# Splitting the last accumulator of an attention kernel into its two banks, with ScalarE normalising one and two output tiles moved ahead

## The chip, the cores and the metric

The kernel runs on 1 core of one Trainium2 chip. The metric is device time in microseconds (us) of one execution. Engines: PE multiplies matrices (PEld is its weight load), DVE is VectorE, ACT is ScalarE, POOL is GpSimd, SP issues the transfers. The granted clock was 1.0. Times of different kernels are compared only with runs of the kernel before on the same chip.

## The reference

Attention of a layer-normed x over given key and value caches, times a gate; 32 heads, 2048 queries, 2048 keys, head width 128, model width 512.

```python
xn = layernorm(x)                                   # x: 1 x 2048 x 512
q  = (xn @ wq) as 32 heads of 128
p  = softmax(q k^T / sqrt(128)); o = p v            # k_cache, v_cache: 32 heads x 2048 x 128
s  = o @ wo                                         # 4096 -> 512
g  = silu(relu(xn W_gate) * (xn W_up) @ W_down)
out = x + s * g                                     # bf16
```

## The kernel before

The kernel handles 128 blocks (32 heads times 4 groups of 512 queries). A block has 8 key pairs: two score matmuls (512 columns), one exponential of 128x1024 on ACT, and, three pairs later, eight value matmuls (129 columns; the extra column sums the weights) into two accumulator banks in PSUM. Each finished block is divided by its sums on DVE and transposed by a transfer. The output projection is done in 16 tiles of 128 rows. For the last four heads it is done at the end, "final tiles" 0 to 15: four matmuls on PE, then on DVE a multiply by the gate and an add to a prepared base, then a transfer out. Tiles 0 to 7 are done inside the pair loop, 8 to 15 behind it. Tiles 12 to 15 need the very last block, which PE transposes itself; a transposing transfer takes 2.4 us from issue to landing in the median.

These are the parts that matter; `j` runs over the four 128-query groups, and bank = j // 2. Left out: everything ahead of the last loop.

```python
def emit_PV_tile(gp, tt):
    b, h, Q, p = blk_of(gp)
    pb = gp % NPB
    vb = h % 2
    if tt == 0:
        if p == 0:
            if gp == 0:
                _wait(pe, tok_pool)
            if Q == 0:
                _wait(pe, v_tok(h))
        pe.wait_ge(sem_exp.h, gp + 1)
    t = 2 * p + tt
    for j in range(4):
        bank = j // 2
        if t == 0 and j % 2 == 0:
            _wait(pe, norm_tok[b - 1][bank] if b >= 1 else acc_free[bank])
        o_ap = ps_acc[:, bank, (j % 2) * 256:(j % 2) * 256 + VW]
        ins = pe.matmul(o_ap, PT[pb][:, tt, j * 128:(j + 1) * 128], V_sb[vb][:, t, 0:VW],
                        start=(t == 0 and j % 2 == 0), stop=(t == KT - 1 and j % 2 == 1))
        if b == NBLK - 1 and t == KT - 1 and j == 1:
            tx = sem_pv.sig(ins)
        if t == KT - 1 and j == 3:
            ty = sem_pv.sig(ins)
    if t == KT - 1:
        if Q == QB - 1 and h + 2 < H:
            _wait(sp, ty)
            issue_v(h + 2)
        if b < NBLK - 1:
            ntok = emit_norm_block(b, ty)
            norm_tok[b] = (ntok, ntok)
        else:
            emit_norm_last(b, 0, tx)
            emit_norm_last(b, 1, ty)

def emit_norm_last(b, bank, pvtok):
    h, Q = divmod(b, QB)
    g, hh = divmod(h, G)
    ob = b % NON
    _wait(dve, pvtok)
    o_ap, z_ap = acc_view()
    js = slice(2 * bank, 2 * bank + 2)
    rtok = sem_rz.sig(dve.reciprocal(rz_sb[:, js, :], z_ap[:, js, :]))
    _wait(dve, rtok)
    tok = sem_norm.sig(
        dve.tensor_tensor(Onorm[ob][:, js, :], o_ap[:, js, :],
                          rz_sb[:, js, :].to_broadcast([128, 2, Dh]), ALU.mult))
    emit_last_transposes(hh, Q, ob, bank, tok)
    return tok

# ... (emit_last_transposes only appends to pending_last)
def flush_last_transposes():
    s = ring_acquire()
    for k, (hh, Q, ob, bank, tok) in enumerate(pending_last):
        tp_ps = ps_r[:, 2 * s + k, :].bitcast(BF16)
        _wait(pe, tok)
        ins = None
        for jj in range(2):
            j = 2 * bank + jj
            ins = pe.transpose(tp_ps[:, jj * 128:(jj + 1) * 128], Onorm[ob][:, j, :], ident[:])
        ptok = sem_ptr.sig(ins)
        _wait(act, ptok)
        c0 = Q * NQ + bank * 256
        last_ot[bank] = sem_otc.sig(
            act.copy(OT_store[(NG - 1) % 2][:, hh, c0:c0 + 256], tp_ps[:, 0:256])
        )
    ring_tok[s] = list(last_ot.values())
```

```python
def emit_final_tile(n, bank):
    Q, j = divmod(n, 4)
    if n == 0:
        _wait(pe, wo_tok(gL))
    if j == 0:
        _wait(pe, (sem_tl[Q], sem_tl[Q].n))
    if Q == QB - 1:
        _wait(pe, last_ot[j // 2])
    ins = None
    for hh in range(G):
        ins = pe.matmul(ps_r[:, bank, 0:D], OT_store[gL % 2][:, hh, n * 128:(n + 1) * 128],
                        Wo_sb[gL % 2][:, hh, :], start=(hh == 0), stop=(hh == G - 1))
    otok = sem_op.sig(ins)
    fb = fin_cnt[0] % NFT
    fin_cnt[0] += 1
    _wait(dve, otok)
    _wait(dve, fin_free[fb])
    mtok = sem_opa.sig(
        dve.tensor_tensor(fin_tmp[fb][:], ps_r[:, bank, 0:D], g_sb[:, n, :], ALU.mult))
    flush_final_add()
    fin_pending.append((n, fb, mtok))
    return mtok

def flush_final_add():
    if not fin_pending:
        return
    n, fb, mtok = fin_pending.pop()
    Q, j = divmod(n, 4)
    _wait(dve, mtok)
    if n == 0:
        _wait(dve, base_done[NT - 1])
    ftok = sem_opa.sig(
        dve.tensor_tensor(x_sb[:, n, :], x_sb[:, n, :], fin_tmp[fb][:], ALU.add))
    fin_free[fb] = ftok
    if Q == QB - 1 or j % 2 == 1:
        n0 = n if Q == QB - 1 else n - 1
        _wait(sp, ftok)
        sem_out.sig(sp.dma_start(out_t[:, n0:n + 1, :], x_sb[:, n0:n + 1, :]))
```

The PSUM ring that `emit_M` takes its banks from has three slots of two banks. The order at the end of the program is set by these lines; LAG is 3, TOTP 1024, NT 16:

```python
for step in range(LAG, TOTP + LAG):
    gp = step
    gq = step - LAG
    bq, hq, Qq, pq = blk_of(gq)
    items = plan.pop((bq, pq), None)
    if gp < TOTP:
        b, h, Q, p = blk_of(gp)
        if p == 0 and Q == 0:
            sp_head_start(h)
        open_S_pair(gp)
        emit_S_tile(gp, 0)
        if items:
            emit_S_tile(gp, 1)
    if items:
        emit_M(items)
    emit_PV_tile(gq, 0)
    if gp < TOTP and not items:
        emit_S_tile(gp, 1)
    emit_PV_tile(gq, 1)

assert not plan
for n in range(NT - 8, NT - 4, 2):
    emit_M([(emit_final_tile, n), (emit_final_tile, n + 1)])
    if n == NT - 8:
        flush_last_transposes()
for n in range(NT - 4, NT, 2):
    emit_M([(emit_final_tile, n), (emit_final_tile, n + 1)])
flush_final_add()
sp.wait_ge(sem_out.h, sem_out.n)
```

The softmax here doesn't subtract the row's maximum and nothing guards it: scores larger than these inputs give would overflow.

## Time and profile before

| | before |
|---|---|
| time, median of 3 runs | 1286.27 us (1286.2 to 1286.35) |
| span of the profiled run | 1284.5 us |
| PE busy | 1266.6 us, 99% |
| DVE busy | 380.5 us, 30% |
| ACT busy | 1001.7 us, 78% |

The page of the kernel before opens with the busy time of each engine, its share of the span and its instructions; its fourth part is the chain of work that ended last, by engine.

```profile
PE 1266.6 (99%) x11813; PEld 835.2 (65%) x12040; DVE 380.5 (30%) x685; ACT 1001.7 (78%) x1109; POOL 13.2 (1%) x25
...
PE 85%; ACT 12%; issue 1%; DVE 1%; DMA 0%; DVEq 0%
```

PE is busy all the time and carries the chain. The change touches only the last 15 us. The timeline lists instructions in order: start, duration, engine, source line, operation, destination <- sources, count. First PE in the tail of the kernel before, from tiles 6 and 7, the last two inside the pair loop:

```profile
1269.96 1.89 PE L774 MATMUL ps_r<-Wo_sb,OT_store 128*128 128x512 bf16 x8
1271.68 1.98 PE L737 MATMUL ps_acc<-V_sb,PT 128*128 128x129 bf16 x32
1273.71 1.67 PE L774 MATMUL ps_r<-Wo_sb,OT_store 128*128 128x512 bf16 x7
1275.22 0.39 PE L709 MATMUL ps_r<-ident,Onorm 128*128 128x128 bf16 x4
1275.45 5.34 PE L774 MATMUL ps_r<-Wo_sb,OT_store 128*128 128x512 bf16 x24
```

L774 is a final tile, L737 the value matmuls, L709 the transposes. Each group starts a little before the end of the one before it: the record of a 512-column matmul lasts 0.379 us, while the next one starts 0.216 us after it. PE has no gap. (The group at 1273.71 has 7 of its 8 records.) DVE in the same stretch:

```profile
1273.59 0.17 DVE L688 RECIPROCAL rz_sb<-ps_acc 128x2 f32<-128x2 f32 x1 [0.60 <-PE ps_acc L737]
1273.79 0.42 DVE L691 TENSOR_TENSOR Onorm<-ps_acc,rz_sb 128x256 bf16<-128x256 f32 x1
1274.13 0.16 DVE L688 RECIPROCAL rz_sb<-ps_acc 128x2 f32<-128x2 f32 x1
1274.33 0.42 DVE L691 TENSOR_TENSOR Onorm<-ps_acc,rz_sb 128x256 bf16<-128x256 f32 x1
1274.67 0.68 DVE L782 TENSOR_TENSOR fin_tmp<-ps_r,g_sb 128x512 bf16<-128x512 f32 x1
1275.26 0.42 DVE L798 TENSOR_TENSOR x_sb<-x_sb,fin_tmp 128x512 bf16<-128x512 bf16 x1
1275.60 0.68 DVE L782 TENSOR_TENSOR fin_tmp<-ps_r,g_sb 128x512 bf16<-128x512 f32 x1
...
1276.53 0.68 DVE L782 TENSOR_TENSOR fin_tmp<-ps_r,g_sb 128x512 bf16<-128x512 f32 x1
...
1281.19 0.69 DVE L782 TENSOR_TENSOR fin_tmp<-ps_r,g_sb 128x512 bf16<-128x512 f32 x1
1281.79 0.75 DVE L798 TENSOR_TENSOR x_sb<-x_sb,fin_tmp 128x512 bf16<-128x512 bf16 x2
```

L688 and L691 are the reciprocals and normalisations of the last block, L782 a final multiply (tile 8 at 1274.67, tile 15 at 1281.19), L798 a final add (the add of one tile follows the multiply of the next). From 1274.67 on DVE starts a tile every 0.93 us, though PE makes one every 0.86 us, so DVE ends its work behind PE: the last multiply starts 0.40 us after PE's end at 1280.79.

### The profile page before, as it was taken

What the parts mean: (1) busy time and instruction counts of PE and PEld (TensorE: products, weight loads), DVE (VectorE), ACT (ScalarE), POOL (GpSimd) and SP (SyncE); (2) the same over time, 40 slices, a digit from 0 to 9 for tenths busy, and PEclk for the clock granted to TensorE, in tenths of its full rate; (3) what the DMA queues carried; (4) which work ended last, traced back from release to release, by engine and by line L of the source; (5) the groups of instructions that cost most, each with busy time, mean ns of one, the idle gap of its engine ahead of it and who ended that gap; (6) DMA issues with size and microseconds to landing.
All of it is one profiled execution on the core that took longest, in us unless ns stands there. A gap on an engine that the chain in (4) does not pass through costs nothing.

```text
span 1284.5 us, 26708 instructions
## 1 busy us (share of the span) xinstructions
PE 1266.6 (99%) x11813; PEld 835.2 (65%) x12040; DVE 380.5 (30%) x685; ACT 1001.7 (78%) x1109; POOL 13.2 (1%) x25
## 2 busy tenths in 40 slices
PE   9999999999999999999999999999999999999998
PEld 5444466676666666666666666666666666666665
DVE  6433311112222222222222222222222222224355
ACT  3322399998888888888888888888888888888884
POOL 2100000000000000000000000000000000000000
PEclk9999999999999999999999999999999999999999
DMA  9600123232222332332221322323323322332202
GB/s 263 131 1 1 22 47 55 60 56 37 36 54 46 71 54 50 55 70 51 54 45 32 67 46 54 55 67 55 55 51 70 54 36 38 51 67 55 49 15 75
DMA packets 240977, 72.13 MB, mean 56 GB/s; under 512 B 227808, under 2 KB 240864, under 8 KB 240864
## 3 DMA queue, kind: packets, MB, share of 16 engines
q1 hardware_dynamic: 240048, 69.76, 28.5%
q8 instruction: 96, 1.57, 0.5%
q10 hardware_dynamic: 816, 0.66, 0.2%
q14 instruction: 17, 0.14, 0.0%
HBM read 32.77 MB, written 2.10 MB: 27 GB/s over the span
## 4 chain that ended last, share of the span: by engine, by line
PE 85%; ACT 12%; issue 1%; DVE 1%; DMA 0%; DVEq 0%
PE ps_acc L737 32%; PE ps_r L640 25%; ACT PT L650 12%; PE ps_r L573 9%; PE ps_r L594 8%; PE ps_acc L506 4%; PE ps_r L487 4%; PE ps_r L483 4%; PE ps_r L774 1%; DVE fin_tmp L782 0%; PE ps_r L397 0%; DMA x_sb<-in_A_x_dram 0%; DVE x_sb L798 0%; ACT gr_sb L449 0%; PE ps_acc L359 0%
## 5 line engine op out<-in xcount | busy, mean ns | idle before, releaser
L650 ACT ACTIVATE PT<-ps_r 128x1024 bf16<-128x1024 f32 x1024 | 952.5, 1054 | 167.7 <-PE ps_r L640 164.9
L737 PE MATMUL ps_acc<-V_sb,PT 128*128 128x129 bf16 x8192 | 776.5, 220 | 10.7
L737 PEld LDWEIGHTS ps_acc<-V_sb,PT 128*128 128x128 bf16 x8192 | 621.1, 98 | 241.7 <-ACT PT L650 3.5
L640 PE MATMUL ps_r<-QT_sb,KT_sb 128*128 128x512 bf16 x1837 | 675.1, 379 | 0.3
L667 DVE RECIPROCAL rz_sb<-ps_acc 128x4 f32<-128x4 f32 x127 | 23.3, 183 | 729.8 <-PE ps_acc L737 729.8
L640 PEld LDWEIGHTS ps_r<-QT_sb,KT_sb 128*128 128x128 bf16 x2048 | 195.0, 98 | 1.1 <-DVE QT_sb L584 0.4
L573 PE MATMUL ps_r<-xnT,Wq_sb 128*128 128x512 bf16 x511 | 130.9, 379 | 0.1
L594 PE MATMUL ps_r<-Wo_sb,OT_store 128*128 128x512 bf16 x447 | 114.4, 379 | 0.1
L584 DVE CAST QT_sb<-ps_r 128x512 bf16<-128x512 f32 x128 | 88.5, 692 | 48.1 <-PE ps_r L573 48.1
L573 PEld LDWEIGHTS ps_r<-xnT,Wq_sb 128*128 128x128 bf16 x512 | 49.9, 97 | 60.6 <-ACT PT L650 27.1
L670 DVE TENSOR_TENSOR Onorm<-ps_acc,rz_sb 128x512 bf16<-128x512 f32 x127 | 87.8, 691 | 4.4
L594 PEld LDWEIGHTS ps_r<-Wo_sb,OT_store 128*128 128x128 bf16 x448 | 43.8, 98 | 52.9 <-ACT PT L650 0.2
L449 ACT ACTIVATE gr_sb<-ps_r 128x512 bf16<-128x512 f32 x56 | 32.9, 595 | 49.6 <-PE ps_r L483 49.1
L607 DVE TENSOR_TENSOR s_acc<-s_acc,ps_r 128x512 f32<-128x512 f32 x96 | 66.0, 687 | 17.4 <-PE ps_r L594 17.4
L455 DVE TENSOR_TENSOR hT<-gr_sb,ps_r 128x512 bf16<-128x512 bf16 x56 | 38.4, 685 | 46.8 <-PE ps_r L487 42.2
L506 PE MATMUL ps_acc<-Wd_sb,hT 128*128 128x512 bf16 x220 | 48.8, 379 | 0.2
L487 PE MATMUL ps_r<-xnT,Wu_sb 128*128 128x512 bf16 x164 | 42.7, 379 | 0.2
L483 PE MATMUL ps_r<-xnT,Wg_sb 128*128 128x512 bf16 x165 | 42.6, 379 | 0.2
L506 PEld LDWEIGHTS ps_acc<-Wd_sb,hT 128*128 128x128 bf16 x224 | 21.9, 98 | 26.4
L514 ACT ACTIVATE sig_sb<-ps_acc 128x512 f32<-128x512 f32 x12 | 7.2, 597 | 29.5 <-PE ps_acc L506 29.5
L487 PEld LDWEIGHTS ps_r<-xnT,Wu_sb 128*128 128x128 bf16 x168 | 16.4, 98 | 19.8
L483 PEld LDWEIGHTS ps_r<-xnT,Wg_sb 128*128 128x128 bf16 x168 | 16.4, 98 | 19.8
(50 smaller groups left out, 181.0 us busy)
## 6 DMA issues: line engine op xcount, KB each, us to landing
V_sb<-in_A_v_cache_dram SPq DMA_DIRECT2D x32, 512.0 KB, 4.8
Wq_sb<-in_A_wq_dram SPq DMA_DIRECT2D x32, 128.0 KB, 2.5
Wo_sb<-in_A_wo_dram SPq DMA_DIRECT2D x8, 512.0 KB, 4.9
OT_store<-Onorm SPq DMA_TRANSPOSE x127, 2.4
Wd_sb<-in_B_W_down_dram SPq DMA_DIRECT2D x1, 1792.0 KB, 14.6
x_sb<-in_A_x_dram SPq DMA_DIRECT2D x3, 512.0 KB, 12.1
out_dram<-x_sb SPq DMA_DIRECT2D x6, 256.0 KB, 2.2
Wg_sb<-in_B_W_gate_dram SPq DMA_DIRECT2D x1, 768.0 KB, 10.3
```

The source lines that it names most:

```text
L455: dve.tensor_tensor(hT[par][:, fc, :], gr_sb[gk][:], ps_r[:, gb + 1, :], ALU.mult)
L483: ins = pe.matmul(ps_r[:, gb, :], Wg_sb[:, c, fs], xT[:, c, xs], start=(c == 0), stop=(c == DC - 1))
L487: ins = pe.matmul(ps_r[:, gb + 1, :], Wu_sb[:, c, fs], xT[:, c, xs], start=(c == 0), stop=(c == DC - 1))
L506: ins = pe.matmul(ps_acc[:, jb, 0:D], hT[par][:, fc, j * 128:(j + 1) * 128], Wd_sb[:, fc, :], start=(fc == 0), stop=(fc == FC - 1))
L573: ins = pe.matmul(ps_r[:, bank, :], Wq_sb[b][:, c, :], xnT[:, c, qs], start=(c == 0), stop=(c == DC - 1))
L584: etok = sem_qpe.sig(dve.tensor_copy(QT_sb[b][:, qs], ps_r[:, bank, :]))
L594: ins = pe.matmul(ps_r[:, bank, 0:D], OT_store[g % 2][:, hh, n * 128:(n + 1) * 128], Wo_sb[g % 2][:, hh, :], start=(hh == 0), stop=(hh == ...
L607: dve.tensor_tensor(s_acc[:, n, :], s_acc[:, n, :], ps_r[:, bank, 0:D], ALU.add)
L640: ins = pe.matmul(ps_r[:, 2 * s + tt, :], KT_sb[h % 2][:, t * 128:(t + 1) * 128], QT_sb[h % 2][:, qs], start=True, stop=True)
L650: act.activation(PT[pb][:], ps_r[:, 2 * s:2 * s + 2, :], ACTF.Exp, scale=scale)
L670: dve.tensor_tensor(Onorm[ob][:], o_ap, rz_sb[:].to_broadcast([128, 4, Dh]), ALU.mult))
L737: ins = pe.matmul(o_ap, PT[pb][:, tt, j * 128:(j + 1) * 128], V_sb[vb][:, t, 0:VW], start=(t == 0 and j % 2 == 0), stop=(t == KT - 1 and j ...
```

## The change

The intent: at the very end, bank 0 (query groups 0 and 1) gets its 12 remaining value matmuls before bank 1, so that its normalisation can start early; ACT, which is out of exponentials by then, does that normalisation in place of DVE; and final tiles 8 and 9 are moved ahead of these value matmuls, tile 10 between them and the transposes, to keep PE busy. The order of the pair loop does not change; the diff of it only takes out the conditions for its last three steps.

```diff
--- before.py
+++ after.py
@@ -686,6 +686,14 @@
             o_ap, z_ap = acc_view()
             js = slice(2 * bank, 2 * bank + 2)
             rtok = sem_rz.sig(dve.reciprocal(rz_sb[:, js, :], z_ap[:, js, :]))
+            if bank == 0:
+                _wait(act, rtok)
+                for j in range(2):
+                    tok = sem_otc.sig(
+                        act.activation(Onorm[ob][:, j, :], o_ap[:, j, :], ACTF.Copy,
+                                       scale=rz_sb[:, j, 0:1]))
+                emit_last_transposes(hh, Q, ob, bank, tok)
+                return tok
             _wait(dve, rtok)
             tok = sem_norm.sig(
                 dve.tensor_tensor(Onorm[ob][:, js, :], o_ap[:, js, :],
@@ -717,7 +725,7 @@
 
         pending_last = []
 
-        def emit_PV_tile(gp, tt):
+        def emit_PV_tile(gp, tt, banks=(0, 1)):
             b, h, Q, p = blk_of(gp)
             pb = gp % NPB
             vb = h % 2
@@ -729,27 +737,24 @@
                         _wait(pe, v_tok(h))
                 pe.wait_ge(sem_exp.h, gp + 1)
             t = 2 * p + tt
-            for j in range(4):
+            for j in range(2 * banks[0], 2 * banks[-1] + 2):
                 bank = j // 2
                 if t == 0 and j % 2 == 0:
                     _wait(pe, norm_tok[b - 1][bank] if b >= 1 else acc_free[bank])
                 o_ap = ps_acc[:, bank, (j % 2) * 256:(j % 2) * 256 + VW]
                 ins = pe.matmul(o_ap, PT[pb][:, tt, j * 128:(j + 1) * 128], V_sb[vb][:, t, 0:VW],
                                 start=(t == 0 and j % 2 == 0), stop=(t == KT - 1 and j % 2 == 1))
-                if b == NBLK - 1 and t == KT - 1 and j == 1:
-                    tx = sem_pv.sig(ins)
-                if t == KT - 1 and j == 3:
+                if t == KT - 1 and j % 2 == 1 and (j == 3 or b == NBLK - 1):
                     ty = sem_pv.sig(ins)
             if t == KT - 1:
+                if b == NBLK - 1:
+                    emit_norm_last(b, banks[0], ty)
+                    return
                 if Q == QB - 1 and h + 2 < H:
                     _wait(sp, ty)
                     issue_v(h + 2)
-                if b < NBLK - 1:
-                    ntok = emit_norm_block(b, ty)
-                    norm_tok[b] = (ntok, ntok)
-                else:
-                    emit_norm_last(b, 0, tx)
-                    emit_norm_last(b, 1, ty)
+                ntok = emit_norm_block(b, ty)
+                norm_tok[b] = (ntok, ntok)
 
         def sp_head_start(h):
             if h + 1 < H:
@@ -831,31 +836,32 @@
         emit_down(QB - 1, hlast)
         glu_done_tok = sem_g.cur()
 
-        for step in range(LAG, TOTP + LAG):
-            gp = step
-            gq = step - LAG
+        for gp in range(LAG, TOTP):
+            gq = gp - LAG
             bq, hq, Qq, pq = blk_of(gq)
             items = plan.pop((bq, pq), None)
-            if gp < TOTP:
-                b, h, Q, p = blk_of(gp)
-                if p == 0 and Q == 0:
-                    sp_head_start(h)
-                open_S_pair(gp)
-                emit_S_tile(gp, 0)
-                if items:
-                    emit_S_tile(gp, 1)
+            b, h, Q, p = blk_of(gp)
+            if p == 0 and Q == 0:
+                sp_head_start(h)
+            open_S_pair(gp)
+            emit_S_tile(gp, 0)
             if items:
+                emit_S_tile(gp, 1)
                 emit_M(items)
             emit_PV_tile(gq, 0)
-            if gp < TOTP and not items:
+            if not items:
                 emit_S_tile(gp, 1)
             emit_PV_tile(gq, 1)
 
         assert not plan
-        for n in range(NT - 8, NT - 4, 2):
-            emit_M([(emit_final_tile, n), (emit_final_tile, n + 1)])
-            if n == NT - 8:
-                flush_last_transposes()
+        emit_M([(emit_final_tile, NT - 8), (emit_final_tile, NT - 7)])
+        for bank in range(2):
+            for gq in range(TOTP - LAG, TOTP):
+                for tt in range(2):
+                    emit_PV_tile(gq, tt, (bank,))
+        emit_M([(emit_final_tile, NT - 6)])
+        flush_last_transposes()
+        emit_M([(emit_final_tile, NT - 5)])
         for n in range(NT - 4, NT, 2):
             emit_M([(emit_final_tile, n), (emit_final_tile, n + 1)])
         flush_final_add()
```

## The prediction

> **What bounds the kernel now.** The page's first part gives PE 1266.6 us busy of a 1284.5 us span (99%), at full granted clock. The chain of waits is PE 85%, ACT 12% (the exponentials, 1054 ns each). The main loop is untouched (instruction order of both builds). The change only reorders the last 13 us, so at most about 1% is at stake, and "within 2%" is nearly certain.
>
> **The tail before (timeline, last 13 us).** PE is never idle: 32 value matmuls from 1271.68 (57 ns apart), output tiles 8 and 9 (four matmuls each, 0.217 us apart, 0.867 us per tile), four transposes at 1275.22, tiles 10 to 15, end 1280.79. There is no stall at the transposes: bank 1's normalisation ended at 1274.75, inside tile 9. DVE is idle 0.60 us before the first reciprocal (1273.59), does two reciprocals and two normalisations (0.16 + 0.42 us each), starts tile 8's multiply at 1274.67, and from there runs without a gap: eight tiles at 0.93 us (multiply 0.69, add 0.42, overlapped by 0.1 each), tile 15's multiply at 1281.19, last add ending 1282.54, then the last output DMA (1.7 us or more to landing). Since DVE needs 0.93 us a tile and PE 0.867, the very end is DVE behind PE by 0.40 us.
>
> **What the change does.**
> - Removes one 128x256 multiply from DVE (0.42 us; with its dependency step about 0.5) and puts two 128x128 scaled copies on ACT, idle after 1271.50. Estimate from 595 ns for 512 and 1054 ns for 1024 columns: about 0.25 us each. The Trainium skill, "ScalarE: Activation LUTs", section on table sets, says that copy is in every set, so no new table load is needed. The built program agrees: two loads in both versions, both early (1.283 us each in the trace).
> - PE does the same matmuls: tiles 8, 9 before the last 24 value matmuls, bank 0's 12 before bank 1's, tile 10 between them and the transposes, tile 11 after. Its sum does not change; it had no idle to remove.
>
> **Replaying the tail (estimates).** Value matmuls of pair 4 from 1271.68; tile 8 done 1273.2, tile 9 at 1274.0; bank 0 done 1274.7, bank 1 1275.4, tile 10 1276.3, transposes issued about 1276.1, tile 11 done 1277.3, tile 15 done 1280.8, as before. DVE: tiles 8, 9 from 1273.2, reciprocal 0 at 1275.1, reciprocal 1 at 1275.45, normalisation of bank 1 done 1276.1; ACT finishes bank 0 at 1275.8. Both arrive just before the transposes, with little slack for bank 1 (0.05 us). DVE then starts tile 10 at 1276.3, waits for tile 11 (the transposes sit between), starts it at 1277.36 and is the limit for the last five tiles: tile 15's multiply at 1277.36 + 4 x 0.93 = 1281.08, against 1281.19. Gain about 0.1 us: the freed DVE time becomes idle time waiting for PE.
>
> **Predicted:** 1286.2 us, 8 in 10 between 1285.2 and 1287.0. Faster by over 2%: 0.003; within 2%: 0.994; slower: 0.003.
>
> **What would show it.** PE still ends at 1280.8 +- 0.2 in the timeline; DVE's last multiply at 1281.0 to 1281.2; new DVE idle (waits view) before tiles 10 and 11, half a microsecond to one in all; ACT's two copies about 0.25 us each with no table load; no PE idle before the transposes.
>
> **What would make it wrong.** A stall at the transposes, if bank 1's reciprocal is queued on DVE behind tile 9's work: up to 0.5 us slower. A hidden table load: about +0.8 us. Activations over 0.35 us each. Run-to-run spread, 0.15 us, exceeds the effect.

## The result, and the profile after

| | before | after |
|---|---|---|
| time, median of 5 runs, same chip | 1286.21 us (1286.2 to 1286.35) | 1286.12 us (1285.34 to 1286.35) |
| ratio | | 0.9999, 95% interval 0.9985 to 1.0012 |
| span of the profiled run | 1284.5 us | 1284.8 us |
| from the first matmul of tile 6 to DVE's last add's end | 12.59 us | 12.51 us |
| from the first matmul of tile 6 to the end of the span | 14.53 us | 14.44 us |

By time the two kernels are the same. The profiled run of after is even 0.3 us longer in span. The last two rows explain the contradiction: the tail became 0.09 us shorter, while its start came later, by 0.41 us (tile 6 starts at 1269.96 us before and 1270.37 after). That offset is all in the first seven microseconds. PE at the start, in the kernel before and then after:

```profile
1.19 3.81 PE L369 MATMUL ps_r<-warm 128*128 128x512 bf16 x10 [1.19 <-DVE warm L234]
5.26 0.38 PE L359 MATMUL ps_acc<-ident,xc_sb 128*128 128x128 bf16 x4 [0.26 <-DVE xc_sb L349]
5.48 0.59 PE L369 MATMUL ps_r<-warm 128*128 128x512 bf16 x2
6.32 0.40 PE L397 MATMUL ps_r<-xcT,Wg_sb 128*128 128x128 bf16 x4 [0.24 <-ACT xcT L364]
```

```profile
1.19 4.45 PE L369 MATMUL ps_r<-warm 128*128 128x512 bf16 x10 [1.19 <-DVE warm L234]
5.43 0.63 PE L359 MATMUL ps_acc<-ident,xc_sb 128*128 128x128 bf16 x4
5.85 0.63 PE L369 MATMUL ps_r<-warm 128*128 128x512 bf16 x2
6.73 0.40 PE L397 MATMUL ps_r<-xcT,Wg_sb 128*128 128x128 bf16 x4 [0.25 <-ACT xcT L364]
```

Nothing in this stretch was changed. The ten warm-up matmuls (L369) took 3.81 us in one and 4.45 in the other, the four transposes after them (L359) 0.38 and 0.63, and the first gate matmul (L397) starts 0.41 us later. From there to tile 6 both kernels take 1263.64 us, to the hundredth (1269.96 - 6.32 and 1270.37 - 6.73). The Trainium skill, "TensorE: Matmul & The Clock Gate", section on the HAM clock gate, says that PE starts at half clock and that the window which decides when it goes up is free-running, so that the number of slow matmuls differs between runs of one kernel. The traces agree: in the first microseconds the weight loads of the warm-up matmuls follow each other every 0.43 us, while later a 512-column matmul is issued every 0.216 us; seven of the nine gaps between the ten were that slow in before, all nine in after; and two profiles of the same changed kernel had the first gate matmul at 6.73 and at 6.21 us. (The granted clock of the profile doesn't show this: it reads 1.00 in the first 3 us of both kernels. The half rate is read from the spacing alone.)

So the profile needs a clock of its own. Below, **tail time** is counted from the first matmul of tile 6, and the **yardstick** is the tail time at which DVE's last add ends. Tail times in the tables are differences taken from the packed traces in nanoseconds and then rounded. Sums of the rounded figures in the views can differ from them by up to 0.02, which is a quarter of the effect studied here: the views give 12.58 for before; the trace gives 12.590. PE in the tail of after:

```profile
1270.37 1.89 PE L779 MATMUL ps_r<-Wo_sb,OT_store 128*128 128x512 bf16 x8
1272.10 0.62 PE L745 MATMUL ps_acc<-V_sb,PT 128*128 128x129 bf16 x8
1272.55 1.89 PE L779 MATMUL ps_r<-Wo_sb,OT_store 128*128 128x512 bf16 x8
1274.28 1.52 PE L745 MATMUL ps_acc<-V_sb,PT 128*128 128x129 bf16 x24
1275.64 1.03 PE L779 MATMUL ps_r<-Wo_sb,OT_store 128*128 128x512 bf16 x4
1276.50 0.39 PE L717 MATMUL ps_r<-ident,Onorm 128*128 128x128 bf16 x4
1276.72 4.48 PE L779 MATMUL ps_r<-Wo_sb,OT_store 128*128 128x512 bf16 x20
```

There is no gap here either: L779 at 1272.55 is tiles 8 and 9, L745 at 1274.28 the 24 value matmuls (both banks), 1275.64 tile 10, 1276.50 the transposes (L717), and from 1276.72 tiles 11 to 15, ending at 1281.20. In tail time that is 10.83 us, and 10.83 before (1280.79 - 1269.96). DVE of after:

```profile
1273.62 0.69 DVE L787 TENSOR_TENSOR fin_tmp<-ps_r,g_sb 128x512 bf16<-128x512 f32 x1 [0.22 <-PE ps_r L779]
...
1275.49 0.16 DVE L688 RECIPROCAL rz_sb<-ps_acc 128x2 f32<-128x2 f32 x1
1275.84 0.17 DVE L688 RECIPROCAL rz_sb<-ps_acc 128x2 f32<-128x2 f32 x1 [0.19 <-PE ps_acc L745]
1276.04 0.42 DVE L699 TENSOR_TENSOR Onorm<-ps_acc,rz_sb 128x256 bf16<-128x256 f32 x1
1276.70 0.69 DVE L787 TENSOR_TENSOR fin_tmp<-ps_r,g_sb 128x512 bf16<-128x512 f32 x1 [0.23 <-PE ps_r L779]
1277.31 0.42 DVE L803 TENSOR_TENSOR x_sb<-x_sb,fin_tmp 128x512 bf16<-128x512 bf16 x1
1277.79 0.69 DVE L787 TENSOR_TENSOR fin_tmp<-ps_r,g_sb 128x512 bf16<-128x512 f32 x1
...
1281.53 0.68 DVE L787 TENSOR_TENSOR fin_tmp<-ps_r,g_sb 128x512 bf16<-128x512 f32 x1
1282.13 0.75 DVE L803 TENSOR_TENSOR x_sb<-x_sb,fin_tmp 128x512 bf16<-128x512 bf16 x2
```

The brackets at the end of a line are idle time and what ended it. DVE now waits before tile 8, before the second reciprocal, before tile 10, and by 0.06 us before tile 11 (1277.31 + 0.42 to 1277.79). From tile 11 it runs 0.93 us a tile again, and the last multiply starts at tail time 11.16 (1281.53 - 1270.37), where before had 11.24. ACT's two scaled copies:

```profile
1275.69 0.63 ACT L693 ACTIVATE Onorm<-ps_acc,rz_sb 128x128 bf16<-128x128 f32 x2 [3.77 <-DVE rz_sb L688]
1276.81 0.65 ACT L722 COPY OT_store<-ps_r 128x256 bf16<-128x256 bf16 x2 [0.50 <-PE ps_r L717]
```

They took 0.63 us together, each 0.36 us, with no table load before them.

One reading of the page before has to be taken back. The page of after says this of the busy time and of the chain:

```profile
PE 1279.3 (100%) x12040; PEld 835.6 (65%) x12040; DVE 380.4 (30%) x684; ACT 1002.3 (78%) x1111; POOL 13.3 (1%) x25
...
PE 99%; DVE 0%; ACT 0%; issue 0%
```

Here the chain is all PE; the 12% of ACT is gone. That is not an effect of the change: a second profile of the same changed kernel reads

```profile
PE 1266.6 (99%) x11813; PEld 835.1 (65%) x12040; DVE 380.5 (30%) x684; ACT 1002.3 (78%) x1111; POOL 13.3 (1%) x25
...
PE 86%; ACT 12%; issue 1%; DVE 0%; DMA 0%
```

The difference is the number of PE records, 12040 against 11813. Twelve of the thirteen profiles lack 227 matmul records, and in all twelve ACT has 12 or 13% of the chain; in the one complete profile it has none. So the chain seems to step over to ACT where the matmul before is missing. By the complete profile PE bounds this kernel alone.

### The profile page after: what moved, and what is told of

It is laid out like the page before. It is cut to its first block, busy times and chain, and to the rows that moved or that the text cites. A ratio compares the mean times of both kernels' runs of the same rounds, so it can differ in the third digit from the quotient of the medians.

```text
span 1284.8 us, 26936 instructions
## 1 busy us (share of the span) xinstructions
PE 1279.3 (100%) x12040; PEld 835.6 (65%) x12040; DVE 380.4 (30%) x684; ACT 1002.3 (78%) x1111; POOL 13.3 (1%) x25
## 4 chain that ended last, share of the span: by engine, by line
PE 99%; DVE 0%; ACT 0%; issue 0%
PE ps_acc L745 36%; PE ps_r L640 34%; PE ps_r L573 9%; PE ps_r L594 8%; PE ps_acc L506 4%; PE ps_r L483 4%; PE ps_r L487 4%; PE ps_r L779 1%; PE ps_r L369 0%; PE ps_r L397 0%; DVE fin_tmp L787 0%; DVE x_sb L803 0%; PE ps_acc L359 0%; ACT gr_sb L449 0%; ACT xcT L364 0%
## 5 line engine op out<-in xcount | busy, mean ns | idle before, releaser
L745 PEld LDWEIGHTS ps_acc<-V_sb,PT 128*128 128x128 bf16 x8192 | 621.2, 98 | 241.9 <-ACT PT L650 3.5
L745 PE MATMUL ps_acc<-V_sb,PT 128*128 128x129 bf16 x8192 | 776.7, 220 | 0.0
L640 PE MATMUL ps_r<-QT_sb,KT_sb 128*128 128x512 bf16 x2048 | 754.1, 379 | 0.0
```

Source lines behind the costliest of these rows:

```text
L640: ins = pe.matmul(ps_r[:, 2 * s + tt, :], KT_sb[h % 2][:, t * 128:(t + 1) * 128], QT_sb[h % 2][:, qs], start=True, stop=True)
```

## The experiments

Theory A, mine, as it was before the runs: PE has no idle time to win in the tail, and the end is set by when DVE can start its last unbroken row of tiles. (e2 below made a better form of it necessary.) Rivals: the gain comes from taking 0.42 us off DVE (ACT's part); or it comes from the new order; or there is none, and the tail differs by chance. There were eleven runs: nine new kernels and the two old ones once more. All outputs were correct.

| kernel | PE's end | last multiply starts | yardstick | end of span | median time | before, same chip |
|---|---|---|---|---|---|---|
| before | 10.83 | 11.24 | 12.59 | 14.53 | 1286.21 | |
| r_before_again | 10.83 | 11.24 | 12.59 | 14.51 | 1286.27 | 1286.22 |
| after | 10.83 | 11.16 | 12.51 | 14.44 | 1286.12 | 1286.21 |
| r_after_again | 10.83 | 11.16 | 12.51 | 14.44 | 1285.83 | 1285.90 |
| e1_order_only | 10.93 | 11.26 | 12.60 | 14.53 | 1286.22 | 1285.88 |
| e2_act_only | 10.83 | 11.23 | 12.58 | 14.51 | 1286.24 | 1285.88 |
| e3_transposes_first | 11.64 | 12.04 | 13.39 | 15.31 | 1286.59 | 1285.88 |
| e4_transposes_later | 11.44 | 11.69 | 13.04 | 14.97 | 1286.72 | 1285.88 |
| e5_pool_adds | 10.83 | 10.87 | 12.02 | 15.30 | 1286.98 | 1285.90 |
| e6_before_pool_adds | 10.83 | 10.87 | 12.22 | 15.48 | 1287.29 | 1285.90 |
| e7_pool_adds_halves | 10.84 | 10.95 (half) | 13.00 | 15.12 | 1286.39 | 1285.90 |
| e8_one_pool_add | 10.83 | 10.87 | 12.23 | 14.15 | 1285.67 | 1286.22 |
| e9_before_one_pool_add | 10.83 | 10.91 | 12.26 | 14.19 | 1286.12 | 1286.22 |

The middle columns are tail time in us, from one profile each. Two profiles of one kernel agree within 0.01 us in the yardstick and within 0.02 in the end of the span. The times can't decide between these kernels: all ratios to before lie between 0.9995 and 1.0008, and every interval contains 1. Nine runs of before alone reach from 1285.60 to 1287.09 us.

### r_before_again and r_after_again: what repeats

No edit.

> The kernel before against itself, for the noise of a ratio. Yardstick 12.58 +- 0.02 again; the time up to tile 6 moves by tenths of a microsecond. Ratio within 0.05% of 1.

> The changed kernel once more, to see what repeats. Yardstick 12.51 +- 0.03 again, while the time from the start to tile 6 moves by some tenths of a microsecond as it did between the two profiles (1269.96 and 1270.37). Time within 0.1% of before.

Both yardsticks came again (12.59, 12.51), and the starts moved: tile 6 at 1270.54 us and 1269.90. The ratio of before to itself was 0.9999 with an interval of 0.9987 to 1.0012: a change of 0.01% cannot be seen in it, and the tail's 0.09 us is less than that. The gain is real in the trace and invisible in the time. The rival "chance" is out for the tail.

### e1_order_only

After, with bank 0 normalised on DVE as bank 1 is:

```diff
-            if bank == 0:
-                _wait(act, rtok)
-                for j in range(2):
-                    tok = sem_otc.sig(act.activation(... scale=rz_sb[:, j, 0:1]))
-                emit_last_transposes(hh, Q, ob, bank, tok)
-                return tok
```

> Yardstick: from the first matmul of output tile 6 (PE) to the end of the last add on DVE; before 12.58 us, after 12.51. Here only the new order; DVE normalises bank 0 too. Theory A (mine: PE has no idle to win, the end is set by when DVE can start its last unbroken row of tiles): DVE's extra multiply makes bank 1's normalisation end at 6.28 us on this clock, just after the transposes could start, so PE stalls about 0.1 us and the yardstick is 12.60 +- 0.05, no gain. Theory C (the order is what gained): 12.51. Time within 0.1% of before.

Yardstick 12.60, PE's end 10.93: PE stalled 0.10 us at the transposes, as theory A said. The order alone is worth nothing: the yardstick is 0.01 us later than that of before.

### e2_act_only

Before, with the six lines above added to it; the old order.

> The old order, but ACT normalises bank 0. Theory A: DVE may start tile 8's multiply when PE has finished tile 8 (about 0.1 us earlier) and then runs eight tiles at 0.93 us: yardstick 12.47 +- 0.05, as good as the whole change. Theory C (the order gained): 12.58. Time within 0.1% of before.

Yardstick 12.58, not 12.47. Theory A, as I had it, falls here: DVE was given 0.42 us and ended only 0.01 us earlier. DVE in the tail of this kernel:

```profile
1274.99 0.69 DVE L790 TENSOR_TENSOR fin_tmp<-ps_r,g_sb 128x512 bf16<-128x512 f32 x1 [0.23 <-PE ps_r L782]
...
1275.93 0.68 DVE L790 TENSOR_TENSOR fin_tmp<-ps_r,g_sb 128x512 bf16<-128x512 f32 x1
1276.53 0.41 DVE L806 TENSOR_TENSOR x_sb<-x_sb,fin_tmp 128x512 bf16<-128x512 bf16 x1
1276.94 0.69 DVE L790 TENSOR_TENSOR fin_tmp<-ps_r,g_sb 128x512 bf16<-128x512 f32 x1
```

Tile 8 did start 0.11 us earlier (1274.99 is tail time 4.60, against 4.71), and tile 9 too. But tile 10 starts at 1276.94, tail time 6.55, where before had 6.57: between tiles 9 and 10 the row has a slack of 0.08 us (from 1276.53 DVE could have gone on at 1276.86, 0.33 us later). The transposes stand between these two tiles on PE, and cost it 0.22 us, so DVE catches up with PE at tile 10 and has to wait for it. In the kernel before DVE reached tile 10 within 0.02 us of the moment when PE had it ready. I had called its row unbroken from tile 8, which it was, but its limit was already PE from tile 10 on.

That gives a better form of theory A. Let k be the number of tiles after the last one that DVE takes over straight from PE. DVE then falls behind by the difference of the two periods, 0.935 - 0.863 = 0.072 us, for each of the k tiles (DVE: 1277.79 to 1281.53 is four tiles; PE: from 1276.72, twenty matmuls end at 1281.20, (4.48 - 0.379) / 19 = 0.216 us each), and about 0.04 us pass from PE's end to DVE's start. So the last multiply starts at PE's end + 0.04 + 0.072 k:

| kernel | PE's end | transposes stand ahead of tile | k | sum | measured |
|---|---|---|---|---|---|
| before | 10.83 | 10 | 5 | 11.23 | 11.24 |
| e2_act_only | 10.83 | 10 | 5 | 11.23 | 11.23 |
| after | 10.83 | 11 | 4 | 11.16 | 11.16 |
| e1_order_only | 10.93 | 11 | 4 | 11.26 | 11.26 |
| e3_transposes_first | 11.64 | 10 | 5 | 12.04 | 12.04 |
| e4_transposes_later | 11.44 | 12 | 3 | 11.70 | 11.69 |

The formula was made after these runs, so for them it is a description and no test. With k = 0 (DVE takes the last tile straight from PE) the last multiply starts at 10.87, and that was expected of e5 and e8 below.

### e3_transposes_first and e4_transposes_later: the two places around the chosen one

```diff
 # e3                                             # e4
+        flush_last_transposes()
         emit_M([(emit_final_tile, NT - 6)])       emit_M([(emit_final_tile, NT - 6)])
-        flush_last_transposes()                 -flush_last_transposes()
         emit_M([(emit_final_tile, NT - 5)])       emit_M([(emit_final_tile, NT - 5)])
                                                 +flush_last_transposes()
```

> The changed kernel, with the four transposes straight behind the value matmuls, ahead of tile 10, so nothing hides the normalisation. Theory A: PE stalls about 0.8 to 0.9 us before the transposes, the last matmul ends at about 11.66 instead of 10.83, yardstick 13.35 +- 0.15. If the normalisation were off the path anyway (rival): 12.5. Time up by about 0.85 us against the changed kernel, near the noise.

> The changed kernel, with the transposes behind tiles 10 and 11, so nothing hides ACT's copy of the transposed tile ahead of tile 12. Theory A: PE stalls about 0.45 us before tile 12; yardstick 12.9 +- 0.15. If PE had slack at the end (rival: DVE alone sets the end): 12.5.

In e3 the yardstick rose to 13.39: PE waited 0.65 us for ACT's normalisation of bank 0, the four transposes then ran in one row, and its end went to 11.64, 0.81 later. In e4 it rose to 13.04, within the stated range, though the stall was dearer than I had put it, 0.60 us in PE's end (11.44) and not 0.45. (In both, PE's end moved by 0.16 us more than the idle time in the view, 0.65 and 0.44. That is what a matmul's record outlasts the start of the next one by, 0.379 - 0.216: in a stall this overlap is lost too.) The waits view of e4 (engine, line, tile <- whom it waited for: us in total, times, longest):

```profile
PE ps_r L779 <- ACT OT_store L722: 0.4, 1, 0.4
```

So both the normalisation and the copy of the transposed tile are on PE's path unless a tile hides each of them. The change puts exactly one tile ahead of the transposes and one behind them; one place earlier costs 0.88 us of tail, one later 0.53.

### e5, e6, e7: the final adds on POOL

If the end is PE's end plus DVE's lag, DVE's work per tile has to come down. The adds of tiles 10 to 14 were put on POOL (e5 on after, e6 on before); e7 is e5 with tile 15 in two column halves.

```diff
-            _wait(dve, mtok)
+            onpool = NT - 6 <= n <= NT - 2
+            eng = pool if onpool else dve
+            _wait(eng, mtok)
+            if onpool:
+                _wait(pool, base_done[n])
...
-            ftok = sem_opa.sig(
-                dve.tensor_tensor(x_sb[:, n, :], x_sb[:, n, :], fin_tmp[fb][:], ALU.add))
+            ftok = (sem_pfin if onpool else sem_opa).sig(
+                eng.tensor_tensor(x_sb[:, n, :], x_sb[:, n, :], fin_tmp[fb][:], ALU.add))
 # e7 besides: tile 15's matmuls, multiply and add once for columns 0:256 and once for 256:512
```

> The changed kernel, with the final adds of tiles 10 to 14 on POOL (whose 128x512 bf16 operation took 0.78 us in the trace of before). Theory A: DVE then needs about 0.6 us a tile, less than PE's 0.867, so the last multiply starts when PE ends (10.87 on the yardstick's clock) and the last add ends at 12.0 +- 0.1, half a microsecond better. If something else than DVE's rate sets the end: 12.5. If POOL and DVE slow each other down: between the two or worse. Time 0.5 us less than after, within the noise of single runs.

> The kernel before, with the same adds on POOL and nothing of the change. Theory A: with DVE's row broken up the order of the tail no longer matters: yardstick 12.0 +- 0.1, the same as e5_pool_adds. Rival (the change makes room that only DVE could not use): e5 better than this by 0.1 or more.

> e5_pool_adds with tile 15 in two column halves, so that the last multiply and add are half as wide. Theory A: the last multiply starts at 10.98, the last add ends at 11.75 +- 0.15. Time about 0.8 us less than before.

DVE did what was expected: in e5 and e6 the last multiply starts at 10.87, k = 0, in both orders, and e5's last DVE add ends at 12.02. But POOL did not: its last add ends at 13.03 (e5) and 13.22 (e6), and the tails became longer to the end of the span (15.30 and 15.48). e6's yardstick, 12.22, missed the expected 12.0 for the reason that e7 shows below: its last DVE add began at 1281.97 beside a POOL add and took 0.62 us, not 0.42. POOL in e5:

```profile
1277.48 5.92 POOL L808 TENSOR_TENSOR x_sb<-x_sb,fin_tmp 128x512 bf16<-128x512 bf16 x5 [1238.43 <-DVE fin_tmp L788]
```

Five adds take 5.92 us, 1.15 us in the median, more than PE's 0.863 us a tile. My 0.78 us came from an operation with one tensor input (the layer norm's scale and shift); the add has two. The Trainium skill, "GPSIMD Engine Reference", section "Engine selection", says that two-input operations are about twice as slow there as on VectorE and one-input ones about line rate. Here it was 1.15 against 0.42 us, 2.8 times. I should have looked up the shape of the operation and not only its engine.

In e7 the two adds of half a tile ended at 13.00, not 11.75. The second of them and the POOL add beside it:

```profile
1281.63 1.23 DVE L810 TENSOR_TENSOR x_sb<-x_sb,fin_tmp 128x256 bf16<-128x256 bf16 x1
```

```profile
1281.52 1.20 POOL L810 TENSOR_TENSOR x_sb<-x_sb,fin_tmp 128x512 bf16<-128x512 bf16 x1
```

A DVE add of 256 columns lasts 1.23 us when it starts 0.11 us after a POOL add of 1.20 us, and ends 0.14 us after it. In e5 it was the other way round: the DVE add started first, at 1281.97, and the POOL add from 1282.03 took 1.38 us. The Trainium skill, "SBUF — State Buffer", section "SBUF: two separate sides", says that a GpSimd operation and a DVE operation with two SBUF inputs lock a shared port pair for a whole instruction, and the later one blocks. Both pairs of numbers agree with that, as far as POOL's records go, which are rough. DVE's multiplies, which read PSUM and SBUF, stayed at 0.69 us beside POOL.

So e6's test of the order was spoiled in the yardstick, and was repeated with one add only. What it does show is the start of the last multiply: where DVE keeps up with PE, it is the same in both orders (10.87).

### e8_one_pool_add and e9_before_one_pool_add

```diff
-            onpool = NT - 6 <= n <= NT - 2
+            onpool = n == NT - 3
```

> The changed kernel, with only tile 13's final add on POOL, where one add took 1.15 to 1.26 us in e5 to e7 (five in a row were too many: 1.2 us against PE's 0.867 a tile). Theory A: DVE's row behind tile 11 loses 0.33 us, so the last multiply starts when PE ends, at 10.87, and tiles 14 and 15 are added behind it: yardstick 12.22 +- 0.06, 0.3 us less than after. If POOL's add and DVE's adds hold each other up, as one DVE add of 1.23 us in e7 suggests: 12.3 to 12.8, no gain.

> The kernel before, with tile 13's add on POOL. Theory A: last multiply at 10.89, yardstick 12.24 +- 0.06, the same as e8: once DVE's row is shortened, the order of the tail and ACT's part are worth nothing. Rival (the change leaves DVE with something that this cannot have): e8 better by 0.1.

Yardsticks 12.23 and 12.26, against 12.22 and 12.24 expected. DVE and POOL at the end of e8:

```profile
1280.52 1.34 DVE L788 TENSOR_TENSOR fin_tmp<-ps_r,g_sb 128x512 bf16<-128x512 f32 x2
1281.77 0.75 DVE L808 TENSOR_TENSOR x_sb<-x_sb,fin_tmp 128x512 bf16<-128x512 bf16 x2
```

```profile
1280.35 1.25 POOL L808 TENSOR_TENSOR x_sb<-x_sb,fin_tmp 128x512 bf16<-128x512 bf16 x1 [1241.37 <-DVE fin_tmp L788]
```

The one add takes POOL 1.25 us, out of the way; the multiplies of tiles 14 and 15 run back to back, and the second starts about 0.6 us before the adds at 1281.77, at tail time 10.87, straight after PE. The two orders now differ by 0.03 us in the yardstick and 0.04 at the end of the span, against 0.08 and 0.09 between before and after, so more than half of what the whole change was worth in the yardstick was a way around DVE's lag. The rest looks like lag too: in e9 the last multiply still starts 0.08 us after PE's end (10.91), in e8 0.04. e8 has the shortest tail of all: 14.15 us to the end of the span, 0.38 less than before and 0.29 less than after. By time it is not shown to beat them: median 1285.67 us against 1286.22, ratio 0.9995, interval 0.9982 to 1.0008.

## Why the prediction was right, and where it was wrong

- **The total**: predicted 1286.2 us, measured 1286.12. That is agreement within the noise and proves little; a forecast of no change would have agreed as well. The evidence is in tail time: predicted gain of the last multiply 0.11 us (1281.08 against 1281.19), measured 0.08 (11.16 against 11.24). The mechanism of the replay held; the missing 0.03 us is in its terms: DVE's row from tile 11 starts at 1277.38 and not 1277.36, and its four periods are 0.935 us and not 0.93.
- **"PE had no idle to remove"**: right. PE's end is 10.83 in both. This is why the change could gain nearly nothing: on the critical engine it only permutes work.
- **"starts it at 1277.36"** (tile 11, on the trace of before): right. Measured 1277.79 - 0.41 = 1277.38.
- **"The freed DVE time becomes idle time waiting for PE"**: right, and e2 shows it stronger than I meant: alone, the 0.42 us taken off DVE moved the end by 0.01 us.
- **What the gain was made of**: half stated. The replay has the right hand-over after the change (DVE waits for tile 11, since "the transposes sit between"), but it names the removed multiply first and does not see that the kernel before has such a hand-over too, one tile earlier. e1 and e2 show that neither part alone gains (+0.01 and -0.01 us). Together they move the transposes one tile later without a stall, so DVE has four tiles and not five in which to fall behind: 0.07 us by the formula, 0.08 measured. The step that I had wrong is "from there runs without a gap", read as DVE being the limit from tile 8 on; DVE had no gap, but from tile 10 it could not have gone faster.
- **Idle DVE "before tiles 10 and 11, half a microsecond to one in all"**: wrong in place. It was 0.23 + 0.06 us there; with 0.22 before tile 8 and 0.19 before the second reciprocal the sum is 0.70.
- **ACT's copies "about 0.25 us each"**: too small, 0.36. My estimate came from activations without a per-partition scale. The trace of before had the pair that shows the difference: 597 ns with a constant and 687 ns with a per-partition scale at the same 128x512. The Trainium skill, "ScalarE: Activation LUTs", section "What ACT_TABLE_LOAD costs", says that each such operand adds about 93 ns. 251 + 90 = 341 ns would have been nearer. The prediction lists activations over 0.35 us among what would make it wrong; they were, and it cost nothing, because the second copy ended at 1276.31, 0.19 us before the transposes. The slack was smaller than that: in e3, where PE waited for this copy, it started 0.15 us after the copy's end, which leaves an estimated 0.04 us.
- **No hidden table load, no stall at the transposes**: right. The transposes start at 1276.50, when tile 10's last matmul has been issued (1275.64 + 4 x 0.216). The margin was thin: e1, with DVE's normalisation of bank 1 some 0.2 us later, stalls by 0.10.
- **"Run-to-run spread, 0.15 us"**: wrong. Three runs had shown it; nine runs of before on one chip spread over 1.5 us, most of it, as far as the profiles show, from the first 7 us.
- **The chain "ACT 12%"**: a misreading caused by missing matmul records, which the second profile of after shows.

In two profiles of thirteen (r_before_again and e9) the stretch from the first gate matmul to tile 6 took 0.14 to 0.16 us longer than 1263.64. The views place this at its very start: in r_before_again the second group of gate matmuls waited 0.16 us for the transfer of Wu_sb, and in e9 the first group took 0.37 us to issue in place of 0.23. From the second group on, both take as long as before. Open: the start of e1 was later than any other (first gate matmul at 7.42 us) and waited for a weight transfer; how much of the spread in time comes from transfers and how much from the clock was not separated.

## What to carry to other kernels

When the bounding engine has no gap in a stretch, reordering that stretch can only gain what another engine lags behind it at the end; compute that lag (difference of the two periods times the number of tiles since the last hand-over) before writing the change. A change that frees an engine which is about to wait for the bounding one anyway is worth nothing by itself: look one or two tiles ahead for the next hand-over. For effects under a tenth of a per cent, measure from a common event inside the trace and repeat the profile, because the time of the whole run moves by more.

## What the Trainium skill lacked or had wrong

- "GPSIMD Engine Reference", "Engine selection": about twice as slow for two-input operations is too kind for the add of these runs. A 128x512 bf16 add took 1.15 us on POOL and 0.42 us on DVE, 2.8 times.
- "SBUF — State Buffer", "SBUF: two separate sides": agrees with the runs, but has no duration for a DVE add that is blocked by a POOL add; here a 256-column DVE add that came 0.11 us after a POOL add lasted 1.23 us.
- "ScalarE: Activation LUTs", "What ACT_TABLE_LOAD costs": 186 + 93 + 0.833 x 128 = 386 ns for a 128x128 activation with one per-partition operand; the trace has 364 ns (360 to 368), so the sum is a little high at this width.
- "TensorE: Matmul & The Clock Gate", "The HAM clock gate": nothing wrong: it has the count of slow matmuls and the moment of the transition vary from run to run. The runs add only what that does to a whole kernel: all later work of one kernel starts up to 0.52 us later or earlier (first gate matmul at 6.73 and 6.21 us).
- No page that I read warns that missing matmul records move the chain to another engine; here two profiles of one kernel, without and with 227 missing records of 12040, read PE 99% and PE 86%, ACT 12%.
